# The first tile's k and v in 96-row chunks, three k'v copies moved to VectorE, and a new step table for the first two tiles

## The chip, the cores and the metric

The kernel runs on one core of a Trainium2 chip. The metric is the device time of one execution in microseconds (us), as the median of several runs. Durations of single instructions come from one profiled execution. The engines are named as in the profile: PE is TensorE, DVE is VectorE, ACT is ScalarE, POOL is GpSimd, SP is the engine that issues most DMA transfers.

## The reference

```python
# q, k, v: (8, 8, 576, 64); w_in: (512, 2048); w_out: (2048, 512)
kv  = einsum('bhsd,bhse->bhde', k, v)
out = einsum('bhsd,bhde->bhse', q, kv)
rms = sqrt(mean(out * out, axis=-1, keepdims=True) + 1e-06)
x   = (out / rms * g_norm)          # heads side by side: 4608 tokens x 512
h   = x @ w_in
P   = a[0] + a[1] * h + a[2] * h**2 + a[3] * h**3
Q   = 1.0 + abs(b[0]) * abs(h) + abs(b[1]) * h**2
y   = (P / (Q + 1e-06)) @ w_out     # 4608 x 512
```

Per batch and head, k'v is a 64 x 64 product over 576 positions, q is multiplied by it, the result is normalised over its 64 values, and a two-layer network with a rational activation follows. The weights `w_in` and `w_out` reach the kernel as 64-bit floating point words; everything is computed in 32 bits on the chip.

## The kernel before, in words

**Tiles and slots.** The 4608 tokens are cut into 9 tiles of 512 (`TW`), the 2048 hidden values into 16 chunks of 128 (`NF`). One (tile, chunk) pair is a slot; there are 144, numbered through, so slots 0 to 15 are tile 0 and 16 to 31 tile 1. In a slot, PE computes the chunk's `h` (`gemm1`, L516 or L523), ACT and DVE evaluate the rational function (`v` L531, `u` L532, `q` L534, `u` L535 and L541, the reciprocal through logarithm and exponential L543 and L544, L550, L551, `g` L557), and PE adds `g @ w_out` of the slot two earlier into four accumulators (`gemm2`, L581 or L588).

**Precision.** In tile 0 the first 4 chunks of `h` and the first 12 of `g @ w_out` are multiplied in f32 (L516, L581). Everything else uses three fp32r products: each operand is split into a cast (its high part, L248) and a rest (L268 for weights, L309 for x, L568 for `g`, called `gl`). So casts and rests have to exist before the chunk that first needs them: those of `wi4` for slot 4, of `wo12` for slot 12's `gemm2`, of `wo0` to `wo10` for tile 1.

**The weights.** Each unit, `wi0`, `wi2`, ..., `wo14` (two chunks of 128 together, 1 MB of 64-bit words), is fetched (`fetch_w`, L194) and rebuilt as f32 by steps: `hi` and `lo` scale the two halves of the words (L208 on ACT, L210 on DVE), `shift` (L231) and `or` (L236) work on integers on DVE, `add` (L241) mostly on POOL. Then follow `cast` and `rest`.

**The order.** After the start, a table `first_tiles` lists for every unit which engine does which step at which place. `or D 8e` is the step `or` on DVE in slot 8 at place `e`. The places of a slot come in the order s, h, q, v, e, r, g, z; among them the slot's own work has its fixed place (`v` and `u` before h, `q` and L535 after h, L540 and L541 after q, L543 and L544 after v, L550 and L551 after r, `g` after g). Engines run their instructions in order, so a step that waits holds up all that stands behind it on its engine. `x0` and `x1` are the x of tiles 0 and 1 by head pair, with steps `norm` (L820), `cast` and `rest`. A second table, `fetch_at`, says behind which slot a unit's load is issued on SP.

**The start** (L738 on) is written out by hand, instruction by instruction. Tile 0 is the first 512 rows of batch 0, four pairs of heads. For each pair p, SP loads `first_p` in two parts (L657): k and v as 5 chunks of 128 rows, the 576 positions padded with zeros to 640; and q, with a few constants behind it in the first pair. PE multiplies k'v (`first_kv`, L677, two heads per chunk), ACT copies the two 64 x 64 results from PSUM (`first_kvf`, L682), PE multiplies q by it (`first_o`), ACT squares (`first_sq`), PE takes means (`first_ms`), ACT and DVE form the reciprocal root (`first_r`, `first_newton`, L707 to L715), PE spreads it over rows (`first_rb`, with a pattern `spread` that comes by a DMA on ACT's queue), DVE multiplies (`first_norm`, L728). In between stand the steps of `wi0` and `wi2`, in halves, and some matmuls on zeros (`warm`, L666). `b0abs`, a constant that L534 needs, is made by ACT.

Of the kernel before, what the change touches and what calls it, by code (L numbers as in the profile page):

```python
# [23 lines left out]
def linear_attention_then_rational_ffn(  # L24
    ctx: ExitStack,
    tc: tile.TileContext,
    first: bass.AP,
    kv: bass.AP,
# [626 lines left out]
    for p in range(NPAIR):  # L655
        for part in (slice(0, 10 * P), slice(10 * P, NC0 + 8)):
            nc.sync.dma_start(kvq0[p][:, part], first[p][:, part])  # L657
        if p == 0:
            nc.scalar.dma_start(quarters[:, 1, :, D:P], quarters[:, 0, :, 0:D])
    fetch_w(("wi", 0))  # L660
    for u in (("wi", 2), ("wo", 0), ("wi", 4)):
        fetch_w(u)
# [250 lines left out]
```

## Time and profile before

| what | us |
|---|---|
| runs | 891.30, 891.72, 892.01 |
| median | 891.72 |
| the profiled execution | 890.8 |
| its span, first to last instruction | 889.0 |

The profiled execution is 0.9 us below the median; 1.8 us of it lie outside the span. The granted TensorE clock is 1.00 of full speed in every stretch shown below. A group's row gives busy time, a timeline row the start, the duration, the engine, the line of the kernel, what is written from what, and in brackets how long the engine stood idle before it and what ended that.

### The profile page before, as it was taken

Reading aid. Unit: us, or ns where it says so; the run is one execution under the profiler, and the core shown is the slowest. Engines: PE = TensorE matmul, PEld = TensorE weight load, DVE = VectorE, ACT = ScalarE, POOL = GpSimd, SP = SyncE. Lnnn points to the kernel's source line nnn. Section 1 sums busy time; section 2 is a strip of 40 time slices with the busy share of each in tenths; the row PEclk is TensorE's granted clock in tenths of the full one; section 3 lists DMA queues with packets and bytes.
Section 4 is the critical chain, followed back from the end, with each engine's and each line's share of the span. In section 5 each row is a group of like instructions: output and inputs, shape, how many; then the busy total and the mean of one; then the engine's idle time right before and its main releaser. Section 6 shows DMA issues by size and latency. Waiting matters only on the chain.

```text
span 889.0 us, 12105 instructions
## 1 busy us (share of the span) xinstructions
PE 876.8 (99%) x4368; PEld 690.6 (78%) x4368; DVE 693.9 (78%) x1048; ACT 707.5 (80%) x1167; POOL 329.6 (37%) x267
## 2 busy tenths in 40 slices
PE   8999999999999999999999999999999999999998
PEld 5466568878887888878887888788887887888886
DVE  3999998887876787678866786688767877787875
ACT  5999889877887778877887787778877797778775
POOL 3677563525232333324332423242323333332221
PEclk9999999999999999999999999999999999999999
DMA  9575403201131204110410123020402020201001
GB/s 366 209 266 193 144 2 125 77 14 48 52 111 53 49 1 152 62 47 3 148 55 12 49 77 122 16 49 25 136 25 49 0 72 13 49 0 48 1 1 48
DMA packets 25936, 65.94 MB, mean 74 GB/s; under 512 B 2516, under 2 KB 3540, under 8 KB 25876
## 3 DMA queue, kind: packets, MB, share of 16 engines
q1 hardware_dynamic: 25568, 64.91, 22.3%
q8 instruction: 34, 0.56, 0.3%
q10 hardware_dynamic: 308, 0.27, 0.1%
q14 instruction: 26, 0.21, 0.1%
HBM read 55.59 MB, written 9.57 MB: 73 GB/s over the span
## 4 chain that ended last, share of the span: by engine, by line
PE 81%; DVE 10%; ACT 3%; issue 3%; DMA 2%; POOL 1%; SPq 0%; DVEq 0%; ACTq 0%; POOLq 0%
PE h L523 38%; PE acc L588 37%; PE kvp L398 1%; DVE u L550 1%; DVE q L534 1%; DVE r L551 1%; DMA first<-in_first_dram 1%; DVE wow L236 1%; PE op L425 1%; PE op L426 1%; DVE wiw L236 1%; PE ms L438 1%; DVE g L557 1%; PE op L424 1%; DMA out_dram<-ob 1%
## 5 line engine op out<-in xcount | busy, mean ns | idle before, releaser
L523 PE MATMUL h<-x,wiparts 128*128 128x512 f32 x1680 | 412.6, 394 | 0.4 <-ACT x L248 0.3
L523 PEld LDWEIGHTS h<-x,wiparts 128*128 128x128 f32 x1680 | 312.2, 188 | 75.7 <-DVE u L541 5.9
L568 POOL TENSOR_TENSOR gl<-u,gh 128x512 fp32r<-128x512 f32 x131 | 172.0, 1313 | 437.3 <-ACT gh L567 310.0
L550 DVE SCALAR_TENSOR_TENSOR u<-u,na,r 128x512 f32<-128x512 f32 x143 | 106.7, 746 | 86.6 <-ACT r L544 86.2
L534 DVE SCALAR_TENSOR_TENSOR q<-v,b0abs,h 128x512 f32<-128x512 f32 x143 | 106.2, 743 | 68.7 <-ACT u L532 68.7
L531 ACT ACTIVATE v<-h,b 128x512 f32<-128x512 f32 x143 | 98.5, 689 | 75.8 <-PE h L523 75.5
L588 PE MATMUL acc<-woparts,gh 128*128 128x512 f32 x400 | 124.7, 391 | 0.8 <-DVE woparts L268 0.8
L540 ACT ACTIVATE q<-q 128x512 f32<-128x512 f32 x143 | 90.5, 633 | 43.2 <-DVE q L534 41.8
L588 PE MATMUL acc<-woh,gl 128*128 128x512 f32 x320 | 124.6, 389 | 0.0
L588 PE MATMUL acc<-woh,gh 128*128 128x512 f32 x320 | 124.6, 389 | 0.0
L588 PE MATMUL acc<-wol,gh 128*128 128x512 f32 x320 | 122.2, 389 | 0.0
L532 ACT ACTIVATE u<-h,na 128x512 f32<-128x512 f32 x143 | 111.0, 777 | 0.0
L541 DVE SCALAR_TENSOR_TENSOR u<-u,na,h 128x512 f32<-128x512 f32 x143 | 106.9, 748 | 5.1
L567 ACT CAST gh<-u 128x512 fp32r<-128x512 f32 x131 | 81.3, 621 | 33.2 <-DVE u L557 23.1
L543 ACT ACTIVATE r<-q,bias 128x512 f32<-128x512 f32 x143 | 99.0, 692 | 4.6
L551 DVE SCALAR_TENSOR_TENSOR r<-q,r 128x512 f32<-128x512 f32 x143 | 98.5, 689 | 0.0
L544 ACT ACTIVATE r<-r,bias 128x512 f32<-128x512 f32 x143 | 94.7, 662 | 4.7
L535 DVE TENSOR_TENSOR u<-u,h 128x512 f32<-128x512 f32 x143 | 97.3, 681 | 0.0
L557 DVE SCALAR_TENSOR_TENSOR u<-r,u 128x512 f32<-128x512 f32 x131 | 90.5, 691 | 4.2
L588 PEld LDWEIGHTS acc<-woparts,gh 128*128 128x128 f32 x400 | 74.6, 188 | 17.9 <-ACT r L544 1.6
L588 PE MATMUL acc<-woparts,gl 128*128 128x512 f32 x200 | 78.0, 390 | 0.4 <-POOL gl L568 0.4
L588 PEld LDWEIGHTS acc<-wol,gh 128*128 128x128 f32 x320 | 60.1, 188 | 12.5
(137 smaller groups left out, 888.6 us busy)
## 6 DMA issues: line engine op xcount, KB each, us to landing
kvm<-in_kv_dram SPq DMA_DIRECT2D x18, 640.0 KB
raw_wo<-in_w_out_dram SPq DMA_DIRECT2D x8, 1024.0 KB
qr<-in_qT_dram SPq DMA_DIRECT2D x32, 256.0 KB
rb<-rd SPq DMA_DIRECT2D x32, 256.0 KB
out_dram<-ob SPq DMA_DIRECT2D x16, 512.0 KB
kvm<-in_kv_dram SPq DMA_DIRECT2D x20, 320.0 KB
raw_wi<-in_w_in_dram SPq DMA_DIRECT2D x6, 1024.0 KB
first<-in_first_dram SPq DMA_DIRECT2D x4, 640.0 KB
```

The lines of the kernel that those rows point to most:

```text
L523: PE.matmul(ph, w, f, start=(n == 0), stop=(n == len(order) - 1))
L531: ACT.activation(v, ph, AF.Abs, scale=b1)
L532: ACT.activation(u, ph, AF.Identity, bias=na[:, 2:3], scale=na[:, 3:4])
L534: DVE.scalar_tensor_tensor(q, v, b0abs, ph, ALU.add, ALU.mult)
L535: DVE.tensor_tensor(u, u, ph, ALU.mult)
L541: DVE.scalar_tensor_tensor(u, u, na[:, 1:2], ph, ALU.add, ALU.mult)
L543: ACT.activation(r, q, AF.Ln, bias=bias[:, 2:3], scale=QSC)
L550: DVE.scalar_tensor_tensor(u, u, na[:, 0:1], r, ALU.add, ALU.mult)
L551: DVE.scalar_tensor_tensor(r, q, QEPS, r, ALU.add, ALU.mult)
L557: DVE.scalar_tensor_tensor(g, r, 2.0, u, ALU.subtract, ALU.mult)
L568: POOL.tensor_tensor(gl, u, f32(gh), ALU.subtract)
L588: PE.matmul(acc[t][s], a[:, s * P:(s + 1) * P], w, start=first and j == 0, stop=last and all(k != s for k, _ in order[n + 1:]))
```

## The change

The changed kernel loads the k and v of tile 0 as 6 chunks of 96 rows, which need no zeros: 576 KB (96 x 1536 words) in place of 640 KB (128 x 1280). A pair's k'v then takes 24 small matmuls in place of 20. The q part is 128 x 512 in place of 128 x 520; the constants come as an input of their own, `few`, into a tile `small` (128 x 8, 4 KB), by a DMA on ACT's queue ahead of that of `spread`. In the program the seventh of the first loads now waits for the DMA of `small` and the eighth for that of `spread`. The copies of k'v of pairs 1, 2 and 3 go to DVE, also `b0abs`. The halves of `wi0` and `wi2` are fetched in turns. The order of the start is written anew: three `warm` matmuls on `idle` are gone, one is added ahead of `rb` of pair 1, two ahead of that of pair 2. `fetch_at` moves some loads by one or two slots, and the whole of `first_tiles` is laid anew. Nothing behind slot 27 is edited.

```diff
-    kvq0 = [wpool.tile([P, 14 * P + 8], F32, tag=f"p{3 + p}", name=f"first_{p}") for p in range(NPAIR)]
+    kvq0 = [wpool.tile([P, 16 * P], F32, tag=f"p{3 + p}", name=f"first_{p}") for p in range(NPAIR)]
+    small = const.tile([P, 8], F32, name="small")
...
-        ("wi", 10): "hi D 5r, lo A 6q, shift D 6g, or D 7h, add P 7v, cast D 8s, rest P 8g",
+        ("wi", 10): "hi D 5r, lo A 6q, shift D 6g, or D 6z, add P 6z, cast A 8h, rest P 8g",
-        ("wo", 12): "hi A 10r, lo A 11r, shift D 11v, or D 11g, add D 11z, cast A 12g, rest D 13r",
+        ("wo", 12): "hi A 10r, lo A 12q, shift D 11e, or D 11g, add D 12v, cast A 13s, rest D 13r",
...
+    def fetch_first(p, part):
+        at = (kvq0[p][0:R6, 0:12 * P], kvq0[p][:, 12 * P:16 * P])[part]
+        of = (first[p][0:R6, 0:12 * P], first[p][:, 12 * P:16 * P])[part]
+        nc.sync.dma_start(at, of)
+
+    nc.scalar.dma_start(small, few)
+    nc.scalar.dma_start(quarters[:, 1, :, D:P], quarters[:, 0, :, 0:D])
...
-        for c in range(5):
+        m = kvq0[p][0:R6, 0:12 * P].rearrange("p (w c d) -> p w c d", w=2, c=6)
+        for c in range(6):
...
-    def first_kvf(p):
+    def first_kvf(p, by=ACT):
         for j in range(2):
             js = slice(j * D, (j + 1) * D)
-            ACT.copy(kvf[js, 0, p, js], kvp0[p][js, 0:D])
+            copy(by, kvf[js, 0, p, js], kvp0[p][js, 0:D])
...
-    warm(3, idle)
-    first_kvf(3)
+    first_kvf(3, DVE)
...
-    ACT.activation(b0abs, ab[:, 4:5], AF.Abs)
+    DVE.scalar_tensor_tensor(b0abs, ab[:, 4:5], -1.0, ab[:, 4:5], ALU.mult, ALU.max)
...
+    first_warm(1, 1)
...
-    first_warm(2, 3)
+    first_warm(2, 5)
```

DVE at the start of the program, before: the Newton steps L714 and L715, the halved x of pair 0, the first half of `wi0` scaled, shifted (L231) and or-ed (L236).

```order
L714 SCALAR_TENSOR_TENSOR r_0_165<-ms_0_196,r_0_165 128x128
L715 SCALAR_TENSOR_TENSOR r_164<-r_0_165,r_164 128x128
L210 TENSOR_SCALAR xf_0_149<-op_0_179,ghalf 128x512
L210 TENSOR_SCALAR raw_wi_139<-raw_wi_139 128x512
L231 TENSOR_SCALAR wiw_251<-raw_wi_139 128x512
L714 SCALAR_TENSOR_TENSOR r_0_165<-ms_1_227,r_0_165 128x128
L715 SCALAR_TENSOR_TENSOR r_164<-r_0_165,r_164 128x128
L236 SCALAR_TENSOR_TENSOR wiw_251<-raw_wi_139,wiw_251 128x512
```

The same place after, where the Newton step stands in L729 and L730:

```order
L248 COPY kvf<-kvp_1_185 64x64 x2
L766 SCALAR_TENSOR_TENSOR b0abs<-small 128x1
L729 SCALAR_TENSOR_TENSOR r_0_167<-ms_0_202,r_0_167 128x128
L730 SCALAR_TENSOR_TENSOR r_166<-r_0_167,r_166 128x128
L210 TENSOR_SCALAR xf_0_151<-op_0_183,ghalf 128x512
L248 COPY kvf<-kvp_2_209 64x64 x2
L210 TENSOR_SCALAR raw_wi_141<-raw_wi_141 128x512
L231 TENSOR_SCALAR wiw_260<-raw_wi_141 128x512
L248 COPY kvf<-kvp_3_239 64x64 x2
L236 SCALAR_TENSOR_TENSOR wiw_260<-raw_wi_141,wiw_260 128x512
```

Three pairs of k'v copies and `b0abs` have come in; those of pair 3 stand between the shift and the or of `wi0`, and the Newton step of pair 1 has moved behind the or.

DVE around slot 14, before, from `g` of slot 13 on. `woparts` is the rest of `wo14`, `xf_2` the norm of pair 2 of tile 1, `x_3` a rest of tile 1's x.

```order
L557 SCALAR_TENSOR_TENSOR u_13_1018<-r_13_1027,u_13_1018 128x512
L820 TENSOR_TENSOR xf_2_680<-xf_2_680,rb_1_991 128x512
L534 SCALAR_TENSOR_TENSOR q_14_1058<-v_14_1057,b0abs,h_14_1036 128x512
L535 TENSOR_TENSOR u_14_1059<-u_14_1059,h_14_1036 128x512
L541 SCALAR_TENSOR_TENSOR u_14_1059<-u_14_1059,na,h_14_1036 128x512
L268 TENSOR_TENSOR woparts_1073<-wow_1012,woparts_1073 128x1024
L309 TENSOR_TENSOR x_0_1068<-xf_0_466,x_0_1068 128x512
L550 SCALAR_TENSOR_TENSOR u_14_1059<-u_14_1059,na,r_14_1070 128x512
L551 SCALAR_TENSOR_TENSOR r_14_1070<-q_14_1058,r_14_1070 128x512
L557 SCALAR_TENSOR_TENSOR u_14_1059<-r_14_1070,u_14_1059 128x512
L309 TENSOR_TENSOR x_3_1109<-xf_3_794,x_3_1109 128x512
```

After, from the end of `g` of slot 14 on:

```order
L557 SCALAR_TENSOR_TENSOR u_14_1068<-r_14_1082,u_14_1068 128x512
L309 TENSOR_TENSOR x_3_1113<-xf_3_807,x_3_1113 128x512
L309 TENSOR_TENSOR x_3_1113<-xf_2_693,x_3_1113 128x512
L534 SCALAR_TENSOR_TENSOR q_15_1121<-v_15_1120,b0abs,h_15_1099 128x512
L535 TENSOR_TENSOR u_15_1122<-u_15_1122,h_15_1099 128x512
L541 SCALAR_TENSOR_TENSOR u_15_1122<-u_15_1122,na,h_15_1099 128x512
L268 TENSOR_TENSOR woparts_1133<-wow_1019,woparts_1133 128x1024
L550 SCALAR_TENSOR_TENSOR u_15_1122<-u_15_1122,na,r_15_1136 128x512
```

The norm of pair 2 has left DVE (it is POOL's, at 14q), the rest of `wo14` has moved from slot 14 to slot 15, behind L541, and a second rest of x has come in ahead of slot 15's `q` (it was POOL's).

## Rows read from the trace of the kernel before

**Rows 1.** The head of the page and the busy time, share of the span and number of instructions of each engine.

```profile
span 889.0 us, 12105 instructions
PE 876.8 (99%) x4368; PEld 690.6 (78%) x4368; DVE 693.9 (78%) x1048; ACT 707.5 (80%) x1167; POOL 329.6 (37%) x267
```

**Rows 2.** Busy time by stretch: the stretch and its length in us, then busy us (and number of instructions) of PE, PE's weight loads, DVE, ACT and POOL, then the granted clock, the DMA engines' busy share and GB/s.

```profile
0.00:14.00 14.00, 10.44 (x118) 7.47 (x119) 1.25 (x3) 5.87 (x15) 4.94 (x33) 1.00 0.88 337
14.00:30.00 16.00, 14.65 (x79) 8.44 (x77) 14.90 (x26) 15.01 (x26) 6.60 (x4) 1.00 1.02 393
30.00:60.00 30.00, 29.82 (x120) 15.94 (x120) 29.47 (x37) 27.86 (x45) 24.69 (x16) 1.00 0.59 213
60.00:100.00 40.00, 38.73 (x168) 23.32 (x168) 38.53 (x51) 35.74 (x57) 25.99 (x15) 1.00 0.47 168
100.00:130.00 30.00, 28.94 (x105) 19.19 (x104) 28.62 (x40) 25.42 (x37) 17.49 (x11) 1.00 0.25 71
130.00:140.00 10.00, 9.55 (x56) 6.84 (x55) 8.42 (x12) 8.72 (x15) 3.97 (x4) 1.00 0.20 67
140.00:889.00 749.00, 744.63 (x3730) 609.41 (x3728) 572.76 (x884) 588.92 (x977) 245.92 (x189) 1.00 0.17 52
```

**Rows 3.** What PE waited for between 24 and 140 us: total us, times, the longest.

```profile
PE acc L581 <- POOL wow L241: 1.3, 1, 1.3
PE h L516 <- DVE u L541: 0.9, 1, 0.9
PE acc L588 <- DVE woparts L268: 0.8, 1, 0.8
PE acc L588 <- POOL gl L568: 0.4, 1, 0.4
PE h L523 <- ACT x L248: 0.3, 1, 0.3
```

**Rows 4.** The timeline of the first 30 us: the four k'v groups on PE, the copies of pair 3 on ACT, warm matmuls on PE, and DVE's scalings and shifts up to `q` of slot 0.

```profile
4.61 0.80 PE L677 MATMUL kvp<-first 128*64 128x64 f32 x20
7.86 0.80 PE L677 MATMUL kvp<-first 128*64 128x64 f32 x20 [0.78 <-DMA first<-in_first_dram]
10.24 0.80 PE L677 MATMUL kvp<-first 128*64 128x64 f32 x20
12.47 0.80 PE L677 MATMUL kvp<-first 128*64 128x64 f32 x20 [1.05 <-DMA first<-in_first_dram]
14.86 0.41 ACT L682 COPY kvf<-kvp 64x64 f32<-64x64 f32 x2
21.34 0.83 PE L666 MATMUL rb<-zero 128*128 128x128 f32 x6
14.39 0.43 DVE L210 TENSOR_SCALAR raw_wi<-raw_wi 128x512 f32<-128x512 f32 x1 [2.79 <-DMA raw_wi<-in_w_in_dram]
17.34 0.80 DVE L210 TENSOR_SCALAR raw_wi<-raw_wi 128x512 f32<-128x512 f32 x1 [0.26 <-DMA raw_wi<-in_w_in_dram]
23.75 0.93 DVE L231 TENSOR_SCALAR wiw<-raw_wi 128x512 int32<-128x512 int32 x1
27.92 0.75 DVE L534 SCALAR_TENSOR_TENSOR q<-v,b0abs,h 128x512 f32<-128x512 f32 x1
```

**Rows 5.** What the DMA engines moved from 5 to 11 us (the first loads), and from 108 to 111 us (a stretch in which `rb` is loaded into 64 rows at a time).

```profile
DMA packets 756, 2.43 MB, mean 405 GB/s; under 512 B 98, under 2 KB 98, under 8 KB 756
DMA packets 366, 0.67 MB, mean 224 GB/s; under 512 B 38, under 2 KB 38, under 8 KB 366
```

**Rows 6.** Shift and or on DVE from 30 to 130 us, grouped: busy us and mean ns of one.

```profile
L236 DVE SCALAR_TENSOR_TENSOR wow<-raw_wo,wow 128x1024 int32<-128x1024 int32 x7 | 10.3, 1465 | 0.0
L231 DVE TENSOR_SCALAR wow<-raw_wo 128x1024 int32<-128x1024 int32 x7 | 8.2, 1166 | 0.0
L236 DVE SCALAR_TENSOR_TENSOR wiw<-raw_wi,wiw 128x1024 int32<-128x1024 int32 x6 | 8.0, 1338 | 0.0
L231 DVE TENSOR_SCALAR wiw<-raw_wi 128x1024 int32<-128x1024 int32 x6 | 5.5, 915 | 0.0
```

**Rows 7.** The same two lines by instruction, 24 to 130 us: minimum, median and maximum in ns, and first and last start.

```profile
L231 DVE TENSOR_SCALAR wow<-raw_wo x8: 686/978/2069, 25.3 to 116.6; 128x1024 int32<-128x1024 int32 x8
L236 DVE SCALAR_TENSOR_TENSOR wow<-raw_wo,wow x8: 1212/1226/2337, 26.1 to 119.3; 128x1024 int32<-128x1024 int32 x8
```

**Rows 8.** The timeline around slot 8: DVE's cast of `wi10`, POOL's adds of `wi12` and `wo8`.

```profile
80.87 0.70 DVE L248 CAST wiparts<-wiw 128x1024 fp32r<-128x1024 f32 x1
88.06 2.45 POOL L241 TENSOR_TENSOR wiw<-wiw,raw_wi 128x1024 int32<-128x1024 int32 x1 [3.08 <-issue]
90.47 2.41 POOL L241 TENSOR_TENSOR wow<-wow,raw_wo 128x1024 int32<-128x1024 int32 x1
```

**Rows 9.** The timeline of DVE in slots 12 to 14: slot 12's `u`, the norm of pair 2 of tile 1, the rest of `wo14`, a rest of x.

```profile
114.64 0.75 DVE L550 SCALAR_TENSOR_TENSOR u<-u,na,r 128x512 f32<-128x512 f32 x1 [0.73 <-ACT r L544]
123.53 0.94 DVE L820 TENSOR_TENSOR xf<-xf,rb 128x512 f32<-128x512 f32 x1
126.76 1.23 DVE L268 TENSOR_TENSOR woparts<-wow,woparts 128x1024 fp32r<-128x1024 f32 x1 [0.26 <-ACT woparts L248]
127.91 0.68 DVE L309 TENSOR_TENSOR x<-xf,x 128x512 fp32r<-128x512 f32 x1
```

More of the change, by code (lines that the diff above doesn't have):

```diff
@@ L27, in linear_attention_then_rational_ffn @@
     first: bass.AP,
+    few: bass.AP,
     kv: bass.AP,
@@ L185, in linear_attention_then_rational_ffn, with fetch_w @@
     raws, ups, w32, whl, wparts = {}, {}, {}, {}, {}
-    def fetch_w(u):
+    def fetch_w(u, half=None):
         kind, c = u
-        raws[u] = wpool.tile([P, 2 * DM], I64, tag=raw_room[u], name=f"raw_{kind}{c}")
+        if u not in raws:
+            raws[u] = wpool.tile([P, 2 * DM], I64, tag=raw_room[u], name=f"raw_{kind}{c}")
         src = w_in[c:c + 2].rearrange("c p k f -> p c (k f)") if kind == "wi" else \
@@ L192, in fetch_w @@
         to = raws[u].rearrange("p (c f) -> p c f", c=2)
-        for js in ((slice(0, 1), slice(1, 2)) if u in (("wi", 0), ("wi", 2)) else (slice(0, 2),)):
-            nc.sync.dma_start(to[:, js], src[:, js])
+        js = slice(0, 2) if half is None else slice(half, half + 1)
+        nc.sync.dma_start(to[:, js], src[:, js])
     def words(u, part):
@@ L654, in linear_attention_then_rational_ffn @@
     o0, sq0 = {}, {}
[L655 to L662, printed above, removed]
+    R6 = S // 6
+    def fetch_first(p, part):
[4 more added lines that the diff above has]
+    nc.scalar.dma_start(quarters[:, 1, :, D:P], quarters[:, 0, :, 0:D])
+    fetch_first(0, 0)
+    fetch_first(0, 1)
+    fetch_first(1, 0)
+    fetch_first(1, 1)
+    fetch_first(2, 0)
+    fetch_first(2, 1)
+    fetch_first(3, 0)
+    fetch_first(3, 1)
+    fetch_w(("wi", 0), 0)
+    fetch_w(("wi", 2), 0)
+    fetch_w(("wi", 0), 1)
+    fetch_w(("wi", 2), 1)
+    fetch_w(("wo", 0))
+    fetch_w(("wi", 4))
     def warm(n, on):
@@ L740, in linear_attention_then_rational_ffn @@
     first_o(0)
+    first_kv(1)
     first_sq(0)
-    first_kv(1)
-    first_kvf(1)
+    first_kvf(1, DVE)
     first_ms(0)
-    first_r(0, 1)
     first_o(1)
     first_kv(2)
-    first_sq(1)
-    first_newton(0, 1)
+    first_r(0, 1)
     POOL.tensor_scalar(ghalf, gcol, -0.5, None, ALU.mult)
@@ L752, in linear_attention_then_rational_ffn @@
     POOL.tensor_copy(b1, ab[:, 5:6])
-    first_kvf(2)
+    DVE.scalar_tensor_tensor(b0abs, ab[:, 4:5], -1.0, ab[:, 4:5], ALU.mult, ALU.max)
+    first_newton(0, 1)
     first_x(0, DVE)
+    first_sq(1)
     first_ms(1)
+    first_kv(3)
+    first_kvf(2, DVE)
+    scale_high(("wi", 0), DVE, one)
     first_r(1, 1)
-    first_kv(3)
     first_o(2)
+    conv_b1(("wi", 0), one)
+    first_kvf(3, DVE)
+    scale_low(("wi", 0), ACT, one)
     first_sq(2)
-    scale_high(("wi", 0), DVE, one)
-    conv_b1(("wi", 0), one)
-    warm(3, idle)
-    first_kvf(3)
     first_o(3)
-    scale_low(("wi", 0), ACT, one)
+    first_sq(3)
+    first_rb(0)
+    conv_b2(("wi", 0), one)
+    first_x(2, DVE)
+    first_ms(2)
     first_newton(1, 1)
-    conv_b2(("wi", 0), one)
-    first_sq(3)
-    first_x(2, DVE)
+    first_x(1, ACT)
+    first_ms(3)
+    first_r(2, 2)
+    first_norm(0)
     scale_high(("wi", 2), DVE, one)
-    first_ms(2)
-    first_ms(3)
-    first_x(1, ACT)
-    first_rb(0)
-    conv_b1(("wi", 2), one)
-    ACT.activation(b0abs, ab[:, 4:5], AF.Abs)
-    first_norm(0)
-    first_r(2, 2)
+    scale_low(("wi", 2), ACT, two)
     scale_high(("wi", 0), ACT, two)
     scale_low(("wi", 2), ACT, one)
+    conv_b1(("wi", 2), one)
+    h00 = ps_h.tile([P, TW], F32, tag="h", name="h_0_0")
+    gemm1_part(0, 0, h00, slice(0, TW), (0,))
     first_newton(2, 2)
@@ L783, in linear_attention_then_rational_ffn @@
     conv_b1(("wi", 0), two)
+    first_x(3, ACT)
+    first_warm(1, 1)
     first_rb(1)
+    first_rb(3)
     first_norm(1)
-    h00 = ps_h.tile([P, TW], F32, tag="h", name="h_0_0")
-    gemm1_part(0, 0, h00, slice(0, TW), (0,))
-    scale_low(("wi", 2), ACT, two)
-    first_x(3, ACT)
-    first_rb(3)
     scale_low(("wi", 0), ACT, two)
     first_norm(3)
-    first_warm(2, 3)
-    scale_high(("wo", 0), ACT, both)
+    first_warm(2, 5)
     conv_b2(("wi", 0), two)
     first_rb(2)
+    scale_low(("wo", 0), ACT, both)
+    scale_high(("wi", 2), DVE, two)
+    first_norm(2)
     gemm1_part(0, 0, h00, slice(0, TW), (1,))
-    scale_high(("wi", 2), DVE, two)
-    scale_low(("wo", 0), ACT, both)
-    first_norm(2)
     gemm1_part(0, 0, h00, slice(0, TW), (2,))
+    scale_high(("wo", 0), ACT, both)
     gemm1_part(0, 0, h00, slice(0, TW), (3,))
@@ L869, in linear_attention_then_rational_ffn @@
     finish(NTILE - 1, ph)
-_INS = ["first", "kv", "qT", "w_in", "w_out"]
+_INS = ["first", "few", "kv", "qT", "w_in", "w_out"]
 def kernel(**inputs):
@@ L887 @@
     kv = kv.transpose(0, 1, 3, 4, 2, 5).reshape(B, H // 2, 2, S, 2 * D)
-    kv = _np.concatenate([kv, _np.zeros((B, H // 2, 2, 64, 2 * D), kv.dtype)], axis=3)
+    rows = kv
+    kv = _np.concatenate([rows, _np.zeros((B, H // 2, 2, 64, 2 * D), kv.dtype)], axis=3)
     kv = kv.reshape(B, H // 2, 2, 5, 128, 2 * D).transpose(0, 1, 4, 2, 3, 5)
@@ L893 @@
     few = _np.concatenate([*few, _np.concatenate([g, g]), _np.zeros((128, 1))], axis=1).astype(_np.float32)
-    few = _np.broadcast_to(few, (H // 2, 128, 8))
+    kv6 = _np.zeros((H // 2, 128, 12 * 128), kv.dtype)
+    kv6[:, :S // 6] = rows[0].reshape(H // 2, 2, 6, S // 6, 2 * D).transpose(0, 3, 1, 2, 4).reshape(H // 2, S // 6, -1)
     laid = {
-        "first": _np.concatenate([kv[0].reshape(H // 2, 128, -1), qT[:, :, :512], few], axis=2),
+        "first": _np.concatenate([kv6, qT[:, :, :512]], axis=2),
+        "few": few,
         "kv": kv,
```

22 lines of the change are left out of this document (11 added, 11 removed), and 44 rows, old and new, of the table first_tiles.

## The prediction, made before the changed kernel was run

> **What bounds the kernel now.** I read the page's busy line first: TensorE (PE) works for 99% of the 889.0 us span [rows 1]. Such a kernel gets faster only where PE still waits, so I next read busy time by stretch. From 140 us to the end PE is busy 744.6 of 749 us, and the rows differ from a full engine by gaps of the order of its pipelining; VectorE (DVE) and ScalarE (ACT) have about a quarter and a fifth of their time free there [rows 2]. Nothing the change touches can shorten that stretch; it can only start earlier or later. From 14 to 130 us it is the other way round: DVE is busy 14.9 of 16, 29.5 of 30, 38.5 of 40 and 28.6 of 30 us [rows 2], and PE follows closely behind it. From 0 to 14 us the DMA engines are the full resource (share 0.88 with the start-up in it), DVE has 1.25 us of work.
>
> The list of PE's waits says where this meets the end. Between 24 and 140 us there are five: for `u` of slot 0 (0.9), the add of the words of `wo8` on GpSimd (POOL) (1.3), the rest of `wo12` on DVE (0.8), the x cast (0.3) and `gl` of slot 14 (0.4); together 3.7 us [rows 3]. The one at slot 0 belongs to the start, the other four (2.8) to the table. Since PE hardly waits after 140 us, **a microsecond off a wait in this list is a microsecond off the end**, and a new wait is one on it. That is the whole game: about 3.7 us can be won, 0.4%.
>
> The profiled execution took 890.8 us, its span 889.0; the median of the runs, 891.72, is 0.9 above it. I make the sum as a difference to the profiled execution and apply it to the median.
>
> **The first loads.** The four k'v groups on PE start at 4.61, 7.86, 10.24 and 12.47 us [rows 4]. Each follows its load; the last two gaps are 2.38 and 2.23 us. A pair brings 640 + 260 KB = 921,600 bytes; at the 405 GB/s that the DMA rows show from 5 to 11 us [rows 5] that is 2.28 us, the gap seen. DVE's continuous work begins with the scaling of the first half of `wi0` at 14.39 [rows 4], which waits for a load queued behind the four pairs, so the loads set the start of everything.
>
> Now a pair brings 96 rows of 6,144 bytes (589,824) and 128 x 512 x 4 (262,144). The trace has no 96-row load, so I bound it. At 405 GB/s: 2.10 us a pair, −0.17, and −0.7 for four. From the other side: the only narrow loads, of 64 rows (`rb`), ran at 224 GB/s [rows 5]. If the whole 96-row part ran so, it would take 2.63 and the pair 3.28 us: +1.0, and +4.0 for four. Between them: if only its first 64 rows (393,216 bytes) are held to 224 GB/s and the other 32 pass beside them, it takes 1.76 and the pair 2.40: +0.12, and **+0.5 for four**. I take this one: 96 rows contain the 64 rows that the trace shows slow, and the remaining third has no reason to queue behind them.
>
> [...]
>
> The constants leave the q part (8 columns of it) for a 4 KB load of their own on ACT's queue, ahead of `spread`'s. SP issues in order, and its seventh load now waits for `small`, as its eighth does for `spread`. Behind the seventh stand all later loads, `wi0` first. Six loads are in flight at that time and these two are the smallest, so I cost the wait at nothing; if they landed after the six, a gap before the fourth group would show it.
>
> **The start on DVE.** From 14.39 to `q` of slot 0 at 27.92 it has 13.5 us almost without idle time [rows 2, 4]. The k'v copies of three pairs come onto it. Those of pairs 1 and 2, and `b0abs`, fall before 14.4, where it has 1.25 us of work in 14 us [rows 2]: nothing. Those of pair 3 fall behind it, and they wait for the fourth k'v group, done at 13.3 [rows 4], before DVE comes to them: two copies of 64x64 from PSUM; ACT took 0.41 for the two [rows 4], and I take **+0.4**. In return, two instructions of that stretch were stretched, the scaling at 17.34 (0.80 against 0.43 of the same form at 14.39) and the shift at 23.75 (0.93) [rows 4]. The minimum of the double-sized shift is 0.69 [rows 7], so the half-sized one needs at most about 0.43: together −0.87, if the new order doesn't meet GpSimd. Two more warm matmuls (0.28 each, from 0.83 for three, six passes, at 21.34 [rows 4]) push `rb` of pair 2 and with it the norm that `h_0` waits for: +0.55. The 24 instead of 20 small matmuls of a pair, 0.16 more of 0.80, lie behind the next load. Sum of the start: 0.4 − 0.87 + 0.55 = **+0.1**.
>
> **The table.** What one can win is in the rows of shift and or. On 128x1024 a shift takes 0.69 us and an or 1.21 at the least [rows 7], but from 30 to 130 us they average 1.17 and 1.47 for `wo`, 0.92 and 1.34 for `wi` [rows 6]. Over 26 instructions this is 7 × 0.48 + 7 × 0.25 + 6 × 0.23 + 6 × 0.13 = 7.3 us of pure stretching. The long ones lie beside GpSimd's adds and rests, which work on the same kind of 32-bit tiles in SBUF; that the two engines hinder each other I read from the overlap. The table changes which of them meet. I cannot compute the new meetings; what I can do is follow the content.
>
> At `wo8`: POOL adds `wi12` at 88.06 and `wo8` at 90.47 [rows 8], both at its own rate of 2.4 us, and PE waits 1.3 for the second. The chain ahead of it is DVE's, up to the or of `wi12`. DVE's content up to there changes by one cast out (`wi10`, 0.70 [rows 8]) and one x rest in (0.68 [rows 9]): zero. Half of the stretches before it (some 4 us) may be laid better; I take 1.0 less, so the wait falls to 0.3. From 88 on: the add of `wo12` moves into the 0.73 us in which DVE stands idle ahead of slot 12's `u` [rows 9], and the rest of `wo12` comes that much earlier, about what PE waits for it (0.8). Then the norm of pair 2 (0.94) and the rest of `wo14` (1.23 and 0.26 idle ahead of it) leave DVE's stretch between 123 and 128 us [rows 9]: `g` of slot 14 comes 2.4 us earlier, and the waits for x and for `gl` (0.7) go. Against this, one x rest more (0.68) and the rest of `wo14` now stand in slot 15, behind its `u`: late there next is PE's first matmul on `wo14`, for which I allow +0.8. Sum: −1.0 − 0.8 − 0.7 + 0.8 = **−1.7**. Bounds: −2.8 (all four waits gone, nothing new), and +3.7 (stretching half as much again as 7.3, all of it passed on).
>
> **Sum:** +0.5 + 0.1 − 1.7 = −1.1; 891.72 becomes **890.6 us**. A measurement of this kernel can tell about 0.2% (1.8 us) from no change, so the forecast itself counts as the same.
>
> **Rivals.**
> *Full gain.* The loads run at 405 GB/s (−0.7) and all of the table's waits go (−2.8), start +0.1: −3.4, 888.3 us. For it: the first two pairs land in the DMA engines' saturated rate, whatever the rows; and two of the four waits lie behind moved work. Against it: the narrow row of 224, and slot 15.
> *The stretching is only moved.* Table 0, loads +0.5, start +0.1: 892.3. For it: GpSimd's work is the same and DVE has no idle time to evade it from 30 to 60 us (29.5 of 30). Against it: the moves of `wo12` and `wo14` gain without any of that.
> *Slow first loads.* The 96-row part runs at the rate of the 64-row loads throughout: +4.0 + 0.1 − 1.7 = +2.4, 894.1 us, slower. It outweighs the table's gain from +0.4 a pair on (a 96-row part of 2.03 us, 290 GB/s) and counts as slower from +0.85 (238 GB/s). For it: the 224 GB/s. Against it: a third of its rows lies outside.
>
> **How the numbers follow.** Forecast 0.45 (its own range 889.4 to 891.8; 0.15 of it below −0.2%), full gain 0.25, stretching moved 0.18 (0.05 of it, with longer meetings than before, slower), slow loads 0.12. Faster: 0.15 + 0.25 = 0.40; slower: 0.05 + 0.12 = 0.17; same 0.43. From the full gain with half a microsecond below it to a slow-load case that stops halfway: 887.9 to 893.0.
>
> **What would show it.** Loads: the four k'v groups start no later than 4.6, 8.0, 10.4 and 12.9 us (by the forecast each 0.12 further behind; by full rate the last at 12.0, by slow loads at 15 to 16). Start: scaling of `wi0` at 14.9, `q` of slot 0 at 28.5, stretches at the third and fourth half shift gone. Table: PE's wait for the add of `wo8` below 0.5, those for `wo12`'s rest, x and `gl` of slot 14 gone, one for `wo14`'s rest below 1; mean shift and or of `wo` below 1.1 and 1.4. The forecast is wrong if a PE wait appears that stands nowhere here, most likely in slots 16 to 27, where rests and casts of `wo0` to `wo10` were moved in halves and DVE's spare time is only a quarter.

## The result, and the profile after

The changed kernel takes **896.70 us** (median of 6 runs, 894.43 to 898.00) against 891.63 (6 runs, 891.27 to 892.01) before: a ratio of 1.0055, 95% interval 1.0041 to 1.0068. The forecast was 890.6, in a range from 887.9 to 893.0. The profiled execution took 896.94, its span 895.2, 6.2 more than before.

The timeline of PE's first 22 us, changed kernel (start, duration, engine, line, operation, in brackets the idle time ahead and what ended it):

```profile
5.50 0.92 PE L692 MATMUL kvp<-first 96*64 96x64 f32 x24 [0.75 <-DMA first<-in_first_dram]
8.65 0.92 PE L692 MATMUL kvp<-first 96*64 96x64 f32 x24 [0.56 <-DMA first<-in_first_dram]
11.91 0.92 PE L692 MATMUL kvp<-first 96*64 96x64 f32 x24 [0.57 <-DMA first<-in_first_dram]
14.94 1.39 PE L692 MATMUL kvp<-first 96*64 96x64 f32 x24 [1.75 <-DMA first<-in_first_dram]
19.59 2.04 PE L701 MATMUL op<-first,kvf 128*128 128x512 f32 x2 [1.26 <-issue]
```

What the DMA engines moved from 5 to 11 us, changed kernel:

```profile
DMA packets 471, 1.58 MB, mean 263 GB/s; under 512 B 82, under 2 KB 82, under 8 KB 471
```

The k'v groups are 3.15, 3.26 and 3.03 us apart, where the last two gaps were 2.38 and 2.23 (the first was 3.25) [rows 4], and the rate has fallen from 405 [rows 5] to 263 GB/s. The DMA engines are no less busy for it: their share of this stretch is 1.03, where it was 1.01. The first group is 0.89 us late and the fourth 2.47, each group now waits for its load, and PE's idle time ahead of the fourth is 1.75 us.

Busy time in stretches of 2 us, changed kernel (columns as in [rows 2]; the one after POOL's is the granted clock):

```profile
14.00:16.00 2.00, 1.06 (x23) 1.06 (x24) 0.00 (x0) 0.36 (x2) 0.00 (x0) 0.79 1.07 378
16.00:18.00 2.00, 2.00 (x9) 0.64 (x6) 0.00 (x0) 0.00 (x0) 0.00 (x0) 0.50 1.01 399
22.00:24.00 2.00, 2.00 (x23) 1.64 (x21) 0.62 (x2) 0.84 (x2) 0.00 (x0) 0.50 1.02 406
26.00:28.00 2.00, 2.00 (x19) 1.96 (x18) 1.97 (x5) 2.00 (x4) 0.30 (x1) 1.00 1.02 396
```

After these waits TensorE is granted 0.50 of its clock from about 15 to 25 us; before, the column has 1.00 throughout [rows 2]. The longest of the waits is 1.75 us. That they brought the fall about is my reading of the order in time, no more.

DVE up to `q` of slot 0, changed kernel:

```profile
18.11 0.43 DVE L210 TENSOR_SCALAR raw_wi<-raw_wi 128x512 f32<-128x512 f32 x1 [4.78 <-DMA raw_wi<-in_w_in_dram]
19.03 0.46 DVE L248 COPY kvf<-kvp 64x64 f32<-64x64 f32 x2
23.38 0.69 DVE L743 TENSOR_TENSOR xf<-xf,rb 128x512 f32<-128x512 f32 x1 [1.59 <-PE rb L740]
25.91 0.42 DVE L729 SCALAR_TENSOR_TENSOR r<-ms,r 128x256 f32<-128x256 f32 x1 [1.05 <-ACT r L724]
34.44 0.74 DVE L534 SCALAR_TENSOR_TENSOR q<-v,b0abs,h 128x512 f32<-128x512 f32 x1
```

DVE starts its continuous work at 18.11 instead of 14.39 and then, unlike before, has to wait for PE (1.59) and for a chain that begins on PE (1.05). `q` of slot 0 comes at 34.44 instead of 27.92 [rows 4]: 6.5 us late, a little more than the spans differ. So the table's part in this execution is about zero, and PE's list of waits from 30 to 145 us says why:

```profile
PE acc L588 <- POOL gl L568: 1.7, 2, 0.9
PE acc L588 <- ACT gh L567: 0.7, 1, 0.7
PE acc L588 <- DVE woparts L268: 0.4, 1, 0.4
PE h L516 <- DVE u L541: 0.4, 1, 0.4
```

The waits for `wo8`'s add (1.3) and for the x cast (0.3) of [rows 3] are gone, that for `wo12`'s rest is halved. New is a wait for `gh`, and those for `gl` have grown from 0.4 to 1.7 (`gh` and `gl` are the two parts of `g`); in sum the list has 3.2 us, where it had 3.7. The wait for `gh` and one of the two for `gl` lead to a load. SP's issues before, from 92 to 108 us, where the two of L194 are `wo12` at its start and `wo14` at its end, 99.6:

```profile
92.90 7.09 SPq L194 DMA_DIRECT2D raw_wo<-in_w_out_dram  x2
103.57 1.19 SPq L455 DMA_DIRECT2D rd<-r  x4
105.20 2.65 SPq L463 DMA_DIRECT2D rb<-rd  x4
```

The same in the changed kernel, from 98 to 114 us:

```profile
98.07 0.38 SPq L198 DMA_DIRECT2D raw_wo<-in_w_out_dram  x1
108.74 1.20 SPq L455 DMA_DIRECT2D rd<-r  x4
110.39 1.32 SPq L463 DMA_DIRECT2D rb<-rd  x2
111.81 0.55 SPq L198 DMA_DIRECT2D raw_wo<-in_w_out_dram  x1
112.46 1.23 SPq L463 DMA_DIRECT2D rb<-rd  x2
```

`wo14` moved from slot 10 to slot 11 of `fetch_at`. With that it moved on SP behind `rd` and half of `rb`, the store and loads that belong to tile 1's norm and wait for its root. Before it was issued 4 us ahead of `rd`, now 3 us behind it. What waits for it, changed kernel, ACT and DVE in slot 12:

```profile
119.17 1.20 ACT L208 ACTIVATE raw_wo<-raw_wo 128x1024 f32<-128x1024 f32 x1 [1.91 <-DMA raw_wo<-in_w_out_dram]
```

```profile
121.67 0.75 DVE L550 SCALAR_TENSOR_TENSOR u<-u,na,r 128x512 f32<-128x512 f32 x1 [1.75 <-ACT r L544]
```

ACT's `hi` of `wo14` stands at `12v`, just ahead of the logarithm of slot 12. It waits 1.91 us for the load; behind it stand the logarithm, the exponential, and through them DVE, `g`, its cast, its rest, and PE.

### The profile page after: what moved, and what is told of

Same layout as the page of the kernel before. It is cut to its first block, busy times and chain, and to the rows that moved or that the text cites. A ratio compares the mean times of both kernels' runs of the same rounds, so it can differ in the third digit from the quotient of the medians.

```text
span 895.2 us, 12142 instructions
## 1 busy us (share of the span) xinstructions
PE 880.6 (98%) x4384; PEld 693.1 (77%) x4384; DVE 694.8 (78%) x1058; ACT 707.8 (79%) x1163; POOL 330.3 (37%) x265
## 4 chain that ended last, share of the span: by engine, by line
PE 86%; DVE 6%; DMA 4%; ACT 2%; issue 1%; POOL 0%; ACTq 0%; DVEq 0%; SPq 0%
PE h L523 39%; PE acc L588 37%; PE acc L581 2%; DMA first<-in_first_dram 2%; PE kvp L398 1%; PE h L516 1%; PE op L425 1%; PE op L426 1%; DVE q L534 1%; DMA raw_wo<-in_w_out_dram 1%; PE ms L438 1%; PE op L424 1%; DMA out_dram<-ob 1%; DVE u L550 1%; DVE r L551 1%
## 5 line engine op out<-in xcount | busy, mean ns | idle before, releaser
L541 DVE SCALAR_TENSOR_TENSOR u<-u,na,h 128x512 f32<-128x512 f32 x143 | 106.9, 748 | 5.1
L588 PEld LDWEIGHTS acc<-woh,gh 128*128 128x128 f32 x320 | 60.1, 188 | 12.5
```

The source lines that it names most:

```text
L541: DVE.scalar_tensor_tensor(u, u, na[:, 1:2], ph, ALU.add, ALU.mult)
L588: PE.matmul(acc[t][s], a[:, s * P:(s + 1) * P], w, start=first and j == 0, stop=last and all(k != s for k, _ in order[n + 1:]))
```

## The experiments

Four causes were set against each other. **L**: the 96-row loads are slow, the rest of the start follows. **C**: the clock's half level, 0.50, is a cause of its own. **O**: the new order of the start costs. **W**: `wo14`'s load costs what the table would gain. The runs of before beside these experiments had medians from 890.8 to 891.1.

### The loads alone, both ways

The changed kernel with padded 128-row loads:

```diff
-        at = (kvq0[p][0:R6, 0:12 * P], kvq0[p][:, 12 * P:16 * P])[part]
-        of = (first[p][0:R6, 0:12 * P], first[p][:, 12 * P:16 * P])[part]
+        cs = (slice(0, 10 * P), slice(10 * P, 14 * P))[part]
+        at, of = kvq0[p][:, cs], first[p][:, cs]
...
```

> The changed kernel with the first k and v loaded as before: 5 chunks of 128 rows with the zeros, 20 small matmuls a pair; the constants stay in their own small load, order of the start and table stay as changed. Theory L (the 96-row loads are slow, everything else follows from it): k'v groups at about 4.6, 7.8, 10.2, 12.4 us, the scaling of wi0 at 14.4, TensorE's clock at 1.00 throughout, DVE without its 2.9 us of idle time ahead of q of slot 0, time 890 to 891. Rival C/O (the clock or the new order of the start costs by itself): the groups come early, but the clock still falls to 0.5 or DVE still idles 2 to 3 us before q of slot 0, time 893 to 894.

Measured: 892.44 (889.76 to 894.35, 11 runs), ratio 1.0014 (1.0003 to 1.0025). The start came back: scaling of `wi0` at 13.6, `q` of slot 0 at 27.75. But the median came back only in part, and the runs are 4.6 us apart. In its trace ACT's wait for `wo14` is longer, and PE's after it; the two timelines around slot 12, ACT first:

```profile
113.96 1.15 ACT L208 ACTIVATE raw_wo<-raw_wo 128x1024 f32<-128x1024 f32 x1 [3.44 <-DMA raw_wo<-in_w_out_dram]
```

```profile
119.66 0.76 PE L588 MATMUL acc<-woparts,gh 128*128 128x512 f32 x1 [2.08 <-ACT gh L567]
121.60 0.63 PE L588 MATMUL acc<-woparts,gh 128*128 128x512 f32 x1
```

A matmul takes 0.63 here instead of 0.39: with PE's wait of 2.08 us the granted clock fell to 0.50, as the stretches of the same trace show (granted clock in the column after POOL's):

```profile
118.00:120.00 2.00, 0.34 (x1) 0.26 (x1) 2.00 (x4) 1.57 (x3) 0.32 (x1) 0.93 0.00 0
120.00:122.00 2.00, 1.41 (x3) 0.84 (x3) 1.96 (x3) 1.94 (x4) 0.96 (x1) 0.50 0.00 0
...
124.00:126.00 2.00, 2.00 (x6) 1.54 (x6) 1.97 (x4) 0.64 (x2) 2.00 (x2) 0.50 0.00 0
```

So L holds for the start, but it is not the whole story.

The other way round, the kernel before with 96-row loads only:

```diff
-        for part in (slice(0, 10 * P), slice(10 * P, NC0 + 8)):
-            nc.sync.dma_start(kvq0[p][:, part], first[p][:, part])
+        for rows, part in ((slice(0, 96), slice(0, 12 * P)), (slice(0, P), slice(12 * P, NC0 + 8))):
+            nc.sync.dma_start(kvq0[p][rows, part], first[p][rows, part])
...
```

> The kernel before with only the first k and v loads changed to 6 chunks of 96 rows (and 24 small matmuls); constants, order and table as before. Theory L: the fourth k'v group at about 15.0 instead of 12.5, the scaling of wi0 between 17 and 18; time 2.5 to 3.7 above before (894.2 to 895.4), more if the clock falls as well. Rival (the loads cost little, the rest of the change did it): fourth group below 13.5, time below 893.

Measured: 898.67 (898.56 to 901.65, 5 runs), ratio 1.0088 (1.0075 to 1.0102): 7.8 us slower than before, more than the changed kernel. Its fourth k'v group, DVE's start and `q` of slot 0:

```profile
16.83 1.55 PE L677 MATMUL kvp<-first 96*64 96x64 f32 x24 [1.04 <-DMA first<-in_first_dram]
```

```profile
18.48 0.43 DVE L210 TENSOR_SCALAR raw_wi<-raw_wi 128x512 f32<-128x512 f32 x1 [4.25 <-DMA raw_wi<-in_w_in_dram]
34.71 0.75 DVE L534 SCALAR_TENSOR_TENSOR q<-v,b0abs,h 128x512 f32<-128x512 f32 x1
```

The delay of `wi0`, 4.1 us, is about what L expected, the time is not. `q` of slot 0 is 6.8 us late, 2.7 more than `wi0`. In this execution PE is slow from the first group to about 22 us: a group takes 1.55, where the changed kernel's first three take 0.92. The column of the granted clock does not show it, it has 1.00 there: it counts recorded falls, and what lies ahead of the first record stands as 1.00. That record begins at 4.9 us in the changed kernel's trace, at 4.3 before. Here the matmuls' own durations show the pace: eight of the means (`first_ms`) take 0.66 at 11.05 and at 15.13, and 0.43 at 23.15. So they have to be read at the start. The profiled execution is also the slowest of the five (901.65), and 4.0 of the 10.8 us by which its span is longer come behind `q` of slot 0, where nothing was edited; what they are is not shown.

### The table alone, and `wo14`'s load put back

The kernel before with `first_tiles` and `fetch_at` of the changed kernel:

> The kernel before with only first_tiles and fetch_at from the changed kernel. My term for the table was -1.7: 890.0, with PE's wait for the add of wo8 below 0.5. Rival (the stretching only moves, PE's waits in slots 12 to 14 take the place of the old ones, as the sum of 2.8 in the changed kernel's trace says): 891.7, within 0.5.

Measured: 891.75 (889.12 to 893.98, 12 runs), ratio 1.0007 (0.9996 to 1.0018): no gain, as the rival said. The same wait is in the trace, shorter in this execution, which was the fastest of the twelve (889.12):

```profile
111.58 1.19 ACT L211 ACTIVATE raw_wo<-raw_wo 128x1024 f32<-128x1024 f32 x1 [1.41 <-DMA raw_wo<-in_w_out_dram]
```

Of its runs, the five with a mean granted clock of 0.999 or 1.000 took 889.1 to 891.1, the seven with 0.996 to 0.998 took 891.5 to 894.0. That fits a wait that sometimes costs the clock as well, which these times alone do not show. So one line was changed back:

```diff
-        10: [("wo", 12)],
-        11: [("wo", 14)],
+        10: [("wo", 12), ("wo", 14)],
```

> The kernel before with the changed table and fetch_at, but the load of wo14 issued in slot 10 as before instead of slot 11, where it stands on SP behind the store rd and half of the loads rb of tile 1. Theory W (the table alone loses by that load: ACT waits 1.4 to 3.4 us for it ahead of slot 12's logarithm, PE then waits for gh and gl of slot 12, and after the long ones the granted clock falls to its half level for some us): the load is issued before 100 us, no wait of ACT for wo14, PE's wait for gh of slot 12 is gone and that for gl small; all runs between 888.5 and 890.5, median 889.3 (1.8 below before), clock 0.999 to 1.000. Rival S (the add of wo12 on DVE ahead of slot 12's u is what is late): PE still waits about 1 us at slot 12 and the median stays at 891 or above.

Measured: **887.72** (887.44 to 887.91, 5 runs), ratio 0.9962 (0.9950 to 0.9974). SP, ACT and PE's waits (24 to 140 us) in this kernel:

```profile
97.58 0.37 SPq L196 DMA_DIRECT2D raw_wo<-in_w_out_dram  x1
101.52 1.19 SPq L457 DMA_DIRECT2D rd<-r  x4
103.16 2.65 SPq L465 DMA_DIRECT2D rb<-rd  x4
```

```profile
109.91 1.14 ACT L210 ACTIVATE raw_wo<-raw_wo 128x1024 f32<-128x1024 f32 x1
```

```profile
PE acc L590 <- POOL gl L570: 0.9, 1, 0.9
PE h L518 <- DVE u L543: 0.7, 1, 0.7
PE acc L590 <- DVE woparts L270: 0.4, 1, 0.4
```

The load goes out ahead of `rd`, ACT doesn't wait, `gh` is off the list, and the runs lie within 0.5 us of each other. Theory W holds, and the rival S falls: the add of `wo12` stands ahead of slot 12's `u` here too. One line of `fetch_at` is worth 4.0 us here.

### The start's order alone, and both causes undone

The changed kernel's start with padded loads and the tables of before:

> The changed kernel's start alone: padded 128-row loads, the small load, the new order with the copies on DVE, with fetch_at and the table of before. My term for the start was +0.1: within 0.5 of before, q of slot 0 at 27.5 to 28.3. Rival: the order costs by itself (copies behind the scaling of wi0, one warm-up less), q of slot 0 later than 29, time 1 to 2 above before, or the runs spread over more than 2 us.

Measured: 891.36 (891.16 to 891.89, 11 runs), ratio 1.0002 (0.9993 to 1.0010); `q` of slot 0 at 28.16. Theory O falls.

The changed kernel with both parts undone, padded loads and `wo14` in slot 10:

> The changed kernel with two parts undone: padded 128-row loads, and the load of wo14 in slot 10. By theory L for the start and W for the table: 889 to 889.5, the runs within 1.5 us of each other. If the start's order costs by itself, 890.5 or more; if W is wrong, 891 to 892.5 with runs 4 us apart as with the padded loads alone.

Measured: 888.13 (887.96 to 888.49, 5 runs), ratio 0.9967 (0.9955 to 0.9979), better than expected. And with the 96-row loads left in:

> The changed kernel with one thing undone, the load of wo14 (slot 10 again): 96-row loads, new order, new table. Against the kernel that also has the padded loads (888.1) it prices the 96-row loads alone. Loads as the main cause: fourth k'v group near 15, scaling of wi0 near 18, time 891.5 to 894, 3.5 to 6 above 888.1. Rival (wo14's load was most of the loss of the change): below 891.

Measured: 893.50 (892.33 to 894.00, 7 runs), ratio 1.0027 (1.0016 to 1.0038). These two differ in the loads alone: **+5.4 us**. DVE's start and `q` of slot 0 with 96 rows:

```profile
18.01 0.43 DVE L209 TENSOR_SCALAR raw_wi<-raw_wi 128x512 f32<-128x512 f32 x1 [2.08 <-DMA raw_wi<-in_w_in_dram]
32.13 0.74 DVE L533 SCALAR_TENSOR_TENSOR q<-v,b0abs,h 128x512 f32<-128x512 f32 x1
```

and with 128 rows:

```profile
14.05 0.43 DVE L209 TENSOR_SCALAR raw_wi<-raw_wi 128x512 f32<-128x512 f32 x1 [2.28 <-DMA raw_wi<-in_w_in_dram]
28.17 0.74 DVE L533 SCALAR_TENSOR_TENSOR q<-v,b0abs,h 128x512 f32<-128x512 f32 x1
```

In this pair of traces the delay is 3.96 at both places, and the spans differ by 3.8 (890.5 and 886.7): the loads cost just their lateness. PE was not fast throughout for that. The third and fourth k'v groups with 96 rows:

```profile
13.87 1.55 PE L691 MATMUL kvp<-first 96*64 96x64 f32 x24
15.94 1.04 PE L691 MATMUL kvp<-first 96*64 96x64 f32 x24
```

PE is slow up to about 16 us here and fast behind it; the changed kernel, whose start is the same, had it the other way round, fast to 15 us and at 0.50 of its clock from 15 to 25. There `wi0` is scaled at 18.11, here at 18.01, but `q` of slot 0 comes at 34.44 there and at 32.13 here. So in these two executions the half level behind the fourth group costs 2.2 us of its own, as theory C says; the slow pace ahead of it costs nothing that shows. This was the fastest of the seven runs; the others, up to 1.7 us longer, I put down to the clock (a mean of 0.996 to 0.999), which is argued from the changed kernel's trace and not shown for these runs.

### The clock by itself

```diff
+    warm(3, idle)
     first_kv(1)
...
+    warm(2, idle)
     first_kv(2)
...
+    warm(7, idle)
     first_kv(3)
...
+    warm(6, idle)
     first_o(3)
```

> The changed kernel with matmuls on zeros put into PE's idle time of the start: 3 ahead of the second k'v group, 2 ahead of the third, 7 ahead of the fourth, 6 ahead of the last q product. Theory C (the clock's half level from 15 to 25 us is a cause of its own): the clock stays at 1.00, q of slot 0 comes 2 to 3 us earlier than 34.4, time 893.5 to 894.5. Rival L/O (what is late is the load of wi0 and the chain behind it): the clock stays up but q of slot 0 moves by less than 1 us, time 895.5 or more.

Measured: 894.76 (894.07 to 899.69, 6 runs), ratio 1.0051 (1.0032 to 1.0070), the changed kernel's own ratio. The last two k'v groups:

```profile
16.03 1.31 PE L692 MATMUL kvp<-first 96*64 96x64 f32 x24
19.38 0.92 PE L692 MATMUL kvp<-first 96*64 96x64 f32 x24
```

This doesn't separate C: in this execution PE was slow until about 17 us (a group took 1.55 and 1.31, with 1.00 in the column), and at that pace the added matmuls made the groups late themselves (19.38 instead of 14.94). What there is for C is the pair of traces above, one execution of each.

### Why 96 rows are slow

The same 96 rows, for pairs 1 to 3, in rows 16 to 111 of their tiles:

```diff
+    at0 = (0, 16, 16, 16)
+    for p in range(1, NPAIR):
+        DVE.memset(kvq0[p][:, 0:12 * P], 0.0)
...
-        at = (kvq0[p][0:R6, 0:12 * P], kvq0[p][:, 12 * P:16 * P])[part]
+        at = (kvq0[p][at0[p]:at0[p] + R6, 0:12 * P], kvq0[p][:, 12 * P:16 * P])[part]
...
```

> The changed kernel with the 96 rows of pairs 1, 2 and 3 loaded into rows 16 to 111 of their tiles instead of 0 to 95 (48 rows in either half of the 128); DVE sets these tiles to zero first, and PE multiplies over all 128 rows. Theory H (the load is slow because 64 of its 96 rows lie in one half): the gaps between the k'v groups of pairs 1, 2 and 3 fall from 3.2 to about 2.2 us, fourth group at about 12 to 12.5, scaling of wi0 at 14 to 15, time below 893.5. Rival N (96 rows, or rows of 6 KB, are slow wherever they lie): gaps stay above 3.0, fourth group at 14.5 or later, time 896 to 897.

Measured: 895.57 (893.05 to 897.85, 6 runs), ratio 1.0049 (1.0036 to 1.0061), with a fourth group at 15.82 and this rate from 5 to 11 us:

```profile
DMA packets 468, 1.58 MB, mean 263 GB/s; under 512 B 79, under 2 KB 79, under 8 KB 468
```

The same rate: theory H falls. One rival falls with it, that `wi0` is late because SP issues its load later: here SP issues it at 9.85, in the changed kernel at 11.73, and it is scaled at 17.56 all the same. Then all 128 rows of 6,144 bytes, and 96 rows of 5,120 (one of the six chunks left out), from the kernel with `wo14` in slot 10:

```diff
-        at = (kvq0[p][0:R6, 0:12 * P], kvq0[p][:, 12 * P:16 * P])[part]
+        at = (kvq0[p][:, 0:12 * P], kvq0[p][:, 12 * P:16 * P])[part]
...
```

> As the kernel with wo14's load in slot 10 and 96-row chunks, but all 128 rows of 6,144 bytes are loaded (rows 96 to 127 hold zeros and are not multiplied): 1.05 MB a pair. If the number of rows, 96, is what makes the load slow: rate back at 400 GB/s, gaps between the k'v groups of 2.6 us, in spite of more bytes shorter than the 3.2 of the changed kernel. If rows of 6 KB are slow: 263 GB/s again, gaps of about 4 us.

```diff
-        at = (kvq0[p][0:R6, 0:12 * P], kvq0[p][:, 12 * P:16 * P])[part]
+        at = (kvq0[p][0:R6, 0:10 * P], kvq0[p][:, 12 * P:16 * P])[part]
...
```

> As the kernel with wo14's load in slot 10, with 96 rows but only 5,120 bytes each: the sixth chunk of k and v of tile 0 is neither loaded nor multiplied, so 96 of the 576 positions are left out there. 0.75 MB a pair. If 96 rows are slow: still about 263 GB/s, gaps of 2.9 us. If rows of 6 KB are slow: 400 GB/s, gaps of 1.9 us, fourth group near 11.

The rates from 5 to 11 us, 128 rows of 6,144 bytes:

```profile
DMA packets 739, 2.55 MB, mean 424 GB/s; under 512 B 108, under 2 KB 108, under 8 KB 739
```

and 96 rows of 5,120 bytes:

```profile
DMA packets 556, 1.62 MB, mean 271 GB/s; under 512 B 86, under 2 KB 86, under 8 KB 556
```

It is the number of rows. Loading 32 rows of zeros more makes the load faster, not only its rate: with 128 rows of 6 KB the first half of `wi0` is scaled at 15.39, with 96 rows at 18.01, and the kernel took 889.63 in its one run, against 893.50. A number between:

> As the kernel with wo14's load in slot 10 and 96-row chunks, but 112 rows of 6,144 bytes are loaded (rows 96 to 111 hold zeros and are not multiplied): 0.95 MB a pair. If any number of rows below 128 is loaded slowly: rate from 5 to 11 us at 300 GB/s or less, gaps between the k'v groups of 3.2 us or more. If 96 is a special case: 400 GB/s, gaps of 2.35 us.

```profile
DMA packets 536, 1.85 MB, mean 308 GB/s; under 512 B 84, under 2 KB 84, under 8 KB 536
```

Measured: 890.93 in one run, 308 GB/s: 96 is no special case, 112 rows are slow too. Why the number of rows matters is not shown.

### Leaving the zeros out with 128 rows

The kernel with the start of before, the new table and `wo14` in slot 10 (887.7), four chunks of 128 rows a pair, and the last 64 rows of two pairs in one chunk:

```diff
+        half = slice(p % 2 * D, (p % 2 + 1) * D)
...
+                k, v = (m[:, 0, c, js], m[:, 1, c, js]) if c < 4 else (last[:, 0, js], last[:, 1, js])
...
```

> The kernel with the start of before, the new table and wo14's load in slot 10 (887.7), and the zeros taken out another way: four chunks of 128 rows a pair (128 x 1024 words), and the last 64 rows of two pairs share one load of 128 x 256 words, pair 0 and 2 in rows 0 to 63, pair 1 and 3 in rows 64 to 127; `spread` is loaded behind them in the program. 0.86 MB a pair on 128 rows: at 405 GB/s 2.11 us, 0.16 less than before, fourth group at 11.8 or 11.9 instead of 12.5, time 887.0 to 887.3. Rival (the shorter rows or two loads more eat the gain): fourth group at 12.4 or later, 887.7 or more.

Measured: 889.37 (888.31 to 891.29, 11 runs), ratio 0.9985 (0.9976 to 0.9994), 1.6 us slower than without it (2.0 by the ratios). Its fourth group starts at 11.97, its `wi0` is scaled later, 16.62 against 13.81:

```profile
16.62 0.43 DVE L212 TENSOR_SCALAR raw_wi<-raw_wi 128x512 f32<-128x512 f32 x1 [5.07 <-DMA raw_wi<-in_w_in_dram]
```

The ten first loads keep SP until 10.25, with a wait of 4.6 us for `spread` among them, and the first load of the weights goes out at 10.29. In the trace of before, whose eight first loads this start had, a wait of 4.0 us for `spread` stands ahead of the first load of the weights, which goes out at 9.12. So the order on SP can account for about 1.2 of the 2.8 us at `wi0`; the rest is not explained. So again, with eight loads, the shared rows inside the load of pairs 0 and 2:

```diff
-        for part in (slice(0, 10 * P), slice(10 * P, NC0 + 8)):
+        for part in (slice(0, (10, 8)[p % 2] * P), slice(10 * P, NC0 + 8)):
...
```

> The shared last chunks once more, now with eight first loads instead of ten: the load of pairs 0 and 2 is 128 x 1280 words as before and holds four chunks of its own pair and the last 64 rows of both pairs; that of pairs 1 and 3 is 128 x 1024. No load waits for `spread` ahead of the weights. 0.13 MB less for pairs 1 and 3, 0.32 us each at 405 GB/s: fourth k'v group at 11.2 instead of 11.9, scaling of wi0 at 13.2 instead of 13.8, time 887.1 (0.6 below 887.7). Rival (the earlier load is lost again ahead of q of slot 0, or the engines' lag sets its end): fourth group earlier, but time 887.5 or more.

Measured: ratio 0.9965 (0.9952 to 0.9979), beside 0.9962 without it; five runs lie between 886.89 and 889.41. The profiled one, at a granted clock of 0.85 throughout, took 972.61, so only its loads can be read: the fourth group starts at 11.28 and the scaling of `wi0` at 12.80, as expected or earlier. The time doesn't follow: the rival held. Where the microsecond is lost again stays open.

## Why the prediction was wrong

**What bounds the kernel** was right: from 140 us on PE hardly waits, and what the start and the table win or lose arrives at the end. The spans differ by 6.2, `q` of slot 0 by 6.5. The sign that the prediction named for being wrong, a wait of PE that stands nowhere in it, came with `gh`, though at slot 12 and not in slots 16 to 27.

**The loads: +0.5 was the step that failed first.** The reason given was that "the remaining third has no reason to queue behind" the 64 rows seen slow. The runs don't bear that out: the measured pair of 3.03 to 3.26 us is close to the upper bound (3.28), not the middle (2.40). At 263 GB/s a pair's 851,968 bytes take 3.24 us, and if its q part runs at 405 the 96-row part is left with 2.59 us, 228 GB/s (an estimate), about the 224 of the 64-row loads [rows 5]. The rival of the slow loads named place, size (+4.0) and direction; the loads' lateness was 3.7 at `wi0`, their price with what the clock adds 3.7, 5.4 or 7.8, by the kernel that they stand in. I gave it 0.12, because I trusted a guess at the mechanism over the one narrow load that the trace had. The wait for `small`, put at nothing, is nothing: with padded loads behind it the fourth group starts at 12.13.

**A step that was missing: the clock.** I had not noted that PE's idle time ahead of the fourth group would grow with the delay (1.05 before [rows 4], 1.75 after), nor looked for a fall of TensorE's clock behind it. The granted clock of 0.50 from 16 to 24 us made PE the engine that DVE waits for (1.59 and 1.05). The three warm matmuls that the change takes away stood behind the fourth group, and the clock falls as that group runs (the group starts at 14.94, the fall at 15.2); with padded loads the same order has 1.00 from 14 to 30 us.

**The start: +0.1 was right, in part by luck.** Alone, it gives +0.3 (891.36 to 891.1), which its interval does not tell from nothing. Of the two stretched instructions the scaling takes 0.42 instead of 0.80, but in the two traces of the table with the start of before it takes 0.43 and 0.44, so that stretch was of one execution. The shift of 0.93 takes 0.60, not 0.43, and a Newton step takes 0.56 instead of 0.29, which I had not foreseen.

**The table: −1.7 was too small for the steps and wrong for the change.** The table with `wo14` fetched in slot 10 gives −3.4, the full-gain rival (its −2.8 for the table, and 0.6 more). PE's wait for `wo8` disappears instead of shrinking to 0.3; that for `wo12`'s rest falls to 0.4 instead of nothing; that for `gl` grows to 0.9 instead of going; the one I expected for `wo14`'s rest in slot 15 is not in the list. The mean shift and or of `wo` fall to 1.01 and 1.26 us, as the prediction's signs have it. Of the 3.2 us between the two spans PE's listed waits make 1.7 (3.7 to 2.0), and 0.7 stand already at `q` of slot 0 (27.25 against 27.92), where nothing was edited; the rest I can't place. But the table as changed gives +0.6, nothing that its interval tells from zero. The step that failed is "what I can do is follow the content": I followed DVE and POOL and not SP. `fetch_at` was in the diff, two numbers in the tables were about `wo14` (10 to 11 for its load, 12s to 12v for its `hi`), and the order of SP's rows would have shown `rd` and `rb` between.

**The sum by its parts, as measured:** start +0.3, table −3.4, 96 rows +5.4, `wo14`'s load behind `rd` and `rb` +2.5 (1.0055 against 1.0027 for the kernel in which only this is undone), together +4.8; the change measured +4.9 (0.55% of 891.6). The last two terms are differences along one chain of kernels, so the agreement tests only that the start and the table add up (−3.1; together they measured −2.9). And the prices hang together: the 96 rows cost 3.7 while `wo14` is late, 5.4 with it put back and 7.8 in the kernel before; `wo14`'s load costs 2.5 beside the 96 rows and 4.2 beside padded ones.

## What to carry to other kernels

A transfer that a row count below 128 makes smaller is not therefore faster: here 96 rows took longer than 128 with a third more bytes (264 against 424 GB/s, the first half of `wi0` scaled at 18.01 against 15.39), so padding that fills the partitions can be the cheap form, and the nearest narrow load in the trace is the price to take. A load that moves in a table moves on its queue: list what stands on that queue ahead of it now, above all a store or load that waits for a computation, and which instruction of which engine will be the first to wait for it. And where TensorE's idle time grows by a microsecond or two (here waits of 1.75 and 2.08 us stood ahead of a clock of 0.50), read the granted clock of the next stretch before the end of the sum, and at the start of a trace the duration of a repeated matmul too.
